# Two token blocks of a Strassen-Winograd mixture kernel taken as plain block products, with the weights' sums made afterwards and the fetches in another order

## The chip, the cores and the metric

One Trainium2 chip, and one core of it. The metric is the device time of one execution in microseconds (us), lower is better, as the median of three runs. Engine names are those of the profile: PE multiplies matrices, DVE, ACT and POOL work elementwise, SP issues the transfers.

## What is computed

Three layers follow one another. The first is an attention without softmax, over 8 batches of 8 heads with 576 tokens of 64 values; the other two are dense layers over the 4608 tokens that come out of it.

```python
kv  = einsum('bhsd,bhse->bhde', k, v)
out = einsum('bhsd,bhde->bhse', q, kv)
x   = out / sqrt(mean(out * out, -1) + 1e-6) * g_norm      # to 4608 x 512
h   = x @ w_in                                             # 512 -> 2048
x   = (maximum(h, 0) + alpha * minimum(h, 0)) @ w_out      # 2048 -> 512
out = ((x @ w_a) * (x @ w_b)) @ w_out2                     # 512 -> 1536 -> 512
```

All of it is in 32-bit floats, and the weights reach the chip as 64-bit floats.

## The kernel before, in words

**Products.** Every operand of the dense layers is split in two parts (a rounded one, and what rounding left), and one product of two 128-wide pieces is three matmuls (lines 610 to 613): rounded by rest, rest by rounded, rounded by rounded. On top of that the layers use Strassen and Winograd's scheme: a 2 x 2 block product takes seven products instead of eight, for which sums of the blocks are made of the weights (S1 to S4, lines 504 to 508) and of the tokens (`X.operands`, lines 549 to 585), and the results are added up again outside PE (`first`, lines 590 to 703).

**Units and blocks.** A weight is cut in units of 256 columns: w_in has eight, us1, and they are used in four pairs. The tokens are cut in nine blocks of 512 in the first layer. V (line 805) lists the work: the first layer's nine blocks, each with its four pairs, then the same for w_out and the last layer. One entry of a block and a pair is a piece, and pieces are numbered in the order of V. In the first layer a piece is 7 products x 2 units x 2 halves of the inner dimension x 3 = 84 matmuls of 256 columns, all on line 611.

**A unit's way before its first use.** `Unit.fetch` (line 474) brings 1 MB of 64-bit words in two transfers. `to_float` (line 267) turns each half to floats in one step on ACT (L276), four on DVE (L280, L281, L283, L284) and one on POOL (L286). `combine` (line 501) makes the four sums on DVE (L507), rounds all seven blocks on ACT (L514) and takes the rest on DVE (L516). Only then can PE use the unit. Units of the later weights go the same way, but are stored as floats in device memory by `convert` (line 462) and loaded again by `build` (line 490).

**Attention.** A step is two pairs of heads of one batch; there are 16 steps, and steps 2b and 2b+1 make batch b. On PE a step is `kv` (lines 320, 321), `out` (337, 342) and, after the norm on ACT and DVE (`norm`, line 353), `tr` (390, 394), which puts the tokens in the layout of the dense layers. Steps 0 and 1 leave the first block's tokens in the buffer x[0] and x[1]; the others go through the device-memory tensors xd, from which `X.load` (line 534) fetches a block.

**What sets the order.** Nothing runs in the order of the code. Each operation is a task with an engine, a cost (table COST, line 53), what it reads and writes, and a priority, which is a planned time in us. `Plan.order` (line 120) plays the tasks through on paper and writes down one fixed list for each engine; on the chip each engine takes its list strictly in turn. Transfers are all in SP's list, and one that waits for a buffer or for data holds back those behind it. The priorities come from constants: START is the planned time of the first product, STEP_AT and FETCH_AT place the first four steps and the eight fetches, STEP_IN names the pieces among which the other twelve steps are put, ATT, URGENT, PRELU, BUILD, CONVERT say how much ahead of its use a thing is to be done.

Of the kernel before, what the change touches and what calls it, by code (L numbers as in the profile page):

```python
# [19 lines left out]
P = 128  # L20
# [18 lines left out]
START = 36.0  # L39
ATT = 20.0  # L40
STEP_IN = [2 + 2 * i for i in range(12)]
NFIRST = 4
STEP_AT = [0, 5, 24, 34]
FETCH_AT = [-1, 2, 8, 14, 20, 26, 32, 38]
BUILD, CONVERT = 14.0, 10.0
PRELU = 8.0
PIECES = 2
LAST = 2.5
URGENT = 20.0
# [7 lines left out]
COL128 = 260  # L57
# [20 lines left out]
class Task:  # L78
    __slots__ = ("opts", "fn", "prio", "left", "users", "ready", "end", "eng")


class Plan:
# [37 lines left out]
    def order(self):  # L120
# [10 lines left out]
        out = []  # L131
        while True:
# [12 lines left out]
            x = heapq.heappop(can[e])[1]  # L145
            free[e] = x.end = s + x.opts
# [8 lines left out]
        assert len(out) == len(self.tasks)  # L155
# [4 lines left out]
def body(ctx: ExitStack, tc, kvm, kvt, qt, gn, w_in, alpha, w_o1, w_a, w_b, w_o2, outT):  # L160
# [134 lines left out]
    class Step:  # L295
# [17 lines left out]
        def kv(self, tag):  # L313
# [8 lines left out]
            for s in range(2):  # L322
                task("t", 5 * COL128, lambda s=s: products(s), self.prio, [(self.m[s], 0), (self.tt[s], 0)],
                     [(ps, s)])
# [4 lines left out]
        def out(self, tags):  # L329
# [15 lines left out]
            for s in range(2):  # L345
                task("t", 4 * COL128, lambda s=s: main(s), pr, z + [(self.q[s], 0)], [(p[s], 0)])
                task("a", 512, lambda s=s: nc.scalar.copy(self.o.t[0:CH, s, 0:4], p[s].t[0:CH]), pr, [(p[s], 0)],
                     [(self.o, s)])
            task("t", 2 * COL128, rest, pr, z + [(self.q[0], 0), (self.q[1], 0)], [(p[2], 0)])
# [33 lines left out]
        def tr(self, tags, x=None):  # L383
# [27 lines left out]
            for s in range(2):  # L411
                if x:
# [3 lines left out]
                    dma(32768, lambda s=s: xd[b].t[:, hp + s, 512:SEQ], lambda s=s: y[s].t[:, 512:SEQ], pr,  # L416
# [13 lines left out]

    class Unit:
# [3 lines left out]
        def __init__(self, w, f0, need, second=False):  # L435
            self.w, self.f0, self.need, self.closed, self.dram, self.second = w, f0, need, False, None, second
            self.ab = (1, 512) if second else (2, 256)
# [44 lines left out]
        def direct(self, prio, pieces=1):  # L482
            t = self.words
            self.c = sb("stg", [P, 8, 2, P], 2)
            for i in range(2):
                to_float(*self.cut[i], lambda i=i: self.dst(i), self.permute, [(t, 3 * i), (t, 1), (t, 2)],
                         (self.c, i), prio)
            self.combine(prio, pieces)

        def build(self, key, prio, pieces):  # L490
            self.key = key
            self.c = sb("stg", [P, 8, 2, P], 2)
            for i in range(2):
                dma(262144, lambda i=i: self.dst(i), lambda i=i: self.fit(self.dram.t[:, i]), prio,
                    [(self.dram, i)], [(self.c, i)])
            self.combine(prio, pieces)

        def dst(self, i):
            return self.c.t[:, 4:8:2] if i else self.c.t[:, 0::7]

        def combine(self, prio, pieces=1, engines="v"):
# [4 lines left out]
            for o, f, a, b, r in ops:  # L506
                sub(256, lambda e, o=o, f=f, a=a, b=b: getattr(e, f)(c.t[:, o], c.t[:, a], c.t[:, b]), prio,  # L507
                    r, [(c, {S1: "S1", S2: "S2", S3: "S3", S4: "S4"}[o])], engines)
            reads = [x0, x1, (c, "S1"), (c, "S2"), (c, "S3"), (c, "S4")]
            self.h = slot(self.key, [P, 2, 7, 2, P], F32R)  # L510
            self.pieces = [slice(0, 4), slice(4, 7)] if pieces > 1 else [slice(0, 7)]
            for s in self.pieces:
                k = (s.stop - s.start) * 256
                task("a", k, lambda s=s: nc.scalar.copy(self.h.t[:, 0, s], c.t[:, s]), prio, reads,  # L514
                     [(self.h, s.start)])
                sub(k, lambda e, s=s: e.tensor_sub(self.h.t[:, 1, s], c.t[:, s], f32(self.h.t[:, 0, s])), prio,  # L516
                    reads + [(self.h, s.start)], [(self.h, -1 - s.start)], "v")

        def parts(self, i):
            s = next(s for s in self.pieces if s.start <= i < s.stop)  # L520
            return [(self.h, s.start), (self.h, -1 - s.start)]


    class X:
# [9 lines left out]
        def load(self, prio):  # L534
            t1st, n1 = T1ST[self.la], T1ST[self.la] // 2
            src, size = (x2d, T2ND) if self.la else (xd, SEQ)
            for r in range(2):
                xf, t0, done = self.x[r], self.b * t1st, 0
                while done < t1st:
                    p, o = divmod(t0 + done, size)  # L540
                    m = min(t1st - done, size - o)
# [5 lines left out]
                    done += m  # L547

# [38 lines left out]
    opened = set()  # L587
    RIGHT = [0, 2, 1, 6, 3, 4, 5]

    def first(k, la, units, js, x, odd, late):  # L590
# [9 lines left out]
        def prod(i, bk, new=False):  # L600
# [3 lines left out]
            for u in range(2):  # L604
                w = units[u]

                def go(u=u, w=w):
                    ct = c.t.rearrange("p (m b k t) -> p m b k t", m=m_, b=2, k=2)[:, z]
# [120 lines left out]
    def second(k, la, b, j, n, unit, bk):  # L729
# [20 lines left out]
        for o, i in enumerate(ORDER):  # L750
            def go(i=i):
                for m in range(2):
# [59 lines left out]
    for vi, (la, b, ps) in enumerate(V):  # L812
        for j in (ps if ps is not None else range(8 if la == 0 else 6)):
            pieces.append((vi, j, t))
            t += UNIT2 if ps is None else PAIR[la]
# [5 lines left out]
    for pi, (vi, j, t) in enumerate(pieces):  # L821
        la, b, ps = V[vi]
        for u in ((pairs1, us2)[la][j] if ps is not None else [(wo1, wo2)[la][j]]):
            if u not in need:
# [43 lines left out]
    x.operands(START - 8)  # L868
    for i in range(8):
        us1[i].direct(us1[i].need - 8, 2 if i < 2 else 1)  # L870
# [17 lines left out]
    for pi, (vi, j, t) in enumerate(pieces):  # L888
        la, b, ps = V[vi]
        fst = pi == 0 or pieces[pi - 1][0] != vi  # L890
        if ps is not None:
            units = (pairs1, us2)[la][j]
            end = first(t, la, units, [2 * j, 2 * j + 1] if la == 0 else [j], x, pi % 2,
                        pi > max(at_time.values()) + 2)
# [10 lines left out]
        if pi + 1 < len(pieces) and pieces[pi + 1][0] != vi and V[vi + 1][2] is not None:  # L905
# [3 lines left out]
            x.operands(tn - 9)  # L909
# [32 lines left out]
    for x in plan.order():  # L942
# [47 lines left out]
```

## Time and profile before

| what | us |
|---|---|
| median of the three runs | 1714.66 |
| lowest and highest of them | 1713.45, 1715.16 |
| the profiled execution | 1713.24 |
| span of the profiled execution, first to last instruction | 1711.5 |
| PE busy in the span | 1642.0 (96%) |
| DVE busy in the span | 1331.7 (78%) |
| ACT busy | 750.0 (44%) |
| mean granted PE clock | 0.983 |

The profile is of one execution, and 1.74 us of its time lie outside the span. Times in its rows are counted from the start of the span. A fp32 matmul of the attention shows as two records; a matmul of the products as one. A matmul's busy time overlaps that of the next, so what one costs in a row of them is read from start to start.

### The profile page before, as it was taken

Reading aid. Unit: us, or ns where it says so; the run is one execution under the profiler, and the core shown is the slowest. Engines: PE = TensorE matmul, PEld = TensorE weight load, DVE = VectorE, ACT = ScalarE, POOL = GpSimd, SP = SyncE. Lnnn points to the kernel's source line nnn. Section 1 sums busy time; section 2 is a strip of 40 time slices with the busy share of each in tenths; the row PEclk is TensorE's granted clock in tenths of the full one; section 3 lists DMA queues with packets and bytes.
Section 4 is the critical chain, followed back from the end, with each engine's and each line's share of the span. In section 5 each row is a group of like instructions: output and inputs, shape, how many; then the busy total and the mean of one; then the engine's idle time right before and its main releaser. Section 6 shows DMA issues by size and latency. Waiting matters only on the chain.

```text
span 1711.5 us, 30160 instructions
## 1 busy us (share of the span) xinstructions
PE 1642.0 (96%) x12142; PEld 1632.4 (95%) x12142; DVE 1331.7 (78%) x1789; ACT 750.0 (44%) x929; POOL 153.5 (9%) x105
## 2 busy tenths in 40 slices
PE   5679999999999999999999999999999999999998
PEld 4669999999999999999999999999999999999998
DVE  6886667767769999988898776786667778887885
ACT  4555565556456433333344333333344334333332
POOL 1331012212100000000000101100101100000000
PEclk8789999999999999999999999999999999999999
DMA  8654478665536545445544443342444434444442
GB/s 250 216 174 142 163 237 260 219 223 189 207 124 222 164 158 179 156 159 182 175 137 154 141 164 130 121 163 91 147 142 148 160 130 136 136 148 136 149 136 75
DMA packets 179788, 279.87 MB, mean 164 GB/s; under 512 B 17088, under 2 KB 97472, under 8 KB 179648
## 3 DMA queue, kind: packets, MB, share of 16 engines
q1 hardware_dynamic: 179648, 277.94, 49.3%
q8 instruction: 95, 1.56, 0.4%
q14 instruction: 45, 0.37, 0.1%
HBM read 170.93 MB, written 106.95 MB: 162 GB/s over the span
## 4 chain that ended last, share of the span: by engine, by line
PE 68%; DVE 2%; issue 1%; ACT 1%; DMA 0%; DVEq 0%; ACTq 0%
PE banks L754 34%; PE banks L611 34%; DVE rops L747 1%; DVE fa L776 0%; DVE rl L747 0%; DVE fa L737 0%; ACT rops L571 0%; DVE w L516 0%; DMA fl<-gd 0%; DVE w L737 0%; ACT rops L746 0%; DVE fl L583 0%; ACT fa L621 0%; DVE stg L507 0%; ACT fa L685 0%
## 5 line engine op out<-in xcount | busy, mean ns | idle before, releaser
L611 PE MATMUL banks<-rops,w 128*128 128x256 f32 (+1 forms) x4752 | 701.9, 306 | 22.4 <-ACT w L514 7.2
L611 PEld LDWEIGHTS banks<-rops,w 128*128 128x128 f32 x4752 | 677.3, 193 | 27.2 <-ACT w L514 7.6
L754 PE MATMUL banks<-rops,w 128*128 128x256 f32 x3528 | 432.5, 283 | 3.7 <-DVE rops L747 3.1
L754 PEld LDWEIGHTS banks<-rops,w 128*128 128x128 f32 x3528 | 426.6, 191 | 4.7 <-DVE rops L747 2.9
L621 ACT COPY fa<-banks 128x768 f32<-128x768 f32 (+1 forms) x216 | 156.8, 729 | 334.0 <-PE banks L611 329.3
L611 PE MATMUL banks<-rl,w 128*128 128x384 f32 x1296 | 241.1, 340 | 0.9 <-ACT fa L621 0.9
L611 PEld LDWEIGHTS banks<-rl,w 128*128 128x128 f32 x1296 | 229.4, 188 | 1.2 <-ACT fa L621 1.2
L754 PE MATMUL banks<-rl,w 128*128 128x256 f32 x1764 | 217.5, 280 | 2.2 <-DVE rl L747 1.2
L754 PEld LDWEIGHTS banks<-rl,w 128*128 128x128 f32 x1764 | 212.1, 188 | 2.8 <-DVE rl L747 1.4
L625 DVE TENSOR_TENSOR fa<-fa,banks 128x768 f32<-128x768 f32 (+1 forms) x144 | 127.2, 884 | 77.4 <-PE banks L611 64.7
L746 ACT CAST rops<-fa 128x1792 fp32r<-128x1792 f32 x60 | 101.6, 1696 | 173.3 <-PE banks L754 85.5
L286 POOL TENSOR_TENSOR stg<-stg 128x512 f32<-128x512 f32 x52 | 81.6, 1570 | 958.1 <-DVE stg L284 689.8
L747 DVE TENSOR_TENSOR rops<-fa,rops 128x1792 fp32r<-128x1792 f32 x60 | 124.4, 2077 | 31.1 <-ACT rops L746 31.0
L737 DVE TENSOR_TENSOR fa<-fa 128x256 f32<-128x256 f32 (+1 forms) x267 | 132.8, 520 | 2.5
L689 DVE TENSOR_TENSOR fa<-fa 128x768 f32<-128x768 f32 x72 | 70.9, 985 | 37.1 <-ACT fa L621 36.4
L746 ACT CAST rl<-fa 128x1792 fp32r<-128x1792 f32 x29 | 49.0, 1690 | 108.0 <-PE banks L754 44.3
L685 ACT ACTIVATE fa<-banks,sal_sb 128x512 f32<-128x512 f32 x72 | 46.0, 684 | 93.3 <-PE banks L611 93.3
L697 DVE SCALAR_TENSOR_TENSOR fa<-banks,sgn_sb,fa 128x512 f32<-128x512 f32 x72 | 53.6, 747 | 41.3 <-ACT fa L685 41.0
L697 DVE SCALAR_TENSOR_TENSOR fa<-fa,sgn_sb 128x512 f32<-128x512 f32 x72 | 62.0, 883 | 29.0 <-ACT fa L685 29.0
L516 DVE TENSOR_TENSOR w<-stg,w 128x1792 fp32r<-128x1792 f32 (+2 forms) x50 | 71.2, 1441 | 10.6 <-ACT w L514 10.5
L747 DVE TENSOR_TENSOR rl<-fa,rl 128x1792 fp32r<-128x1792 f32 x29 | 58.7, 2024 | 20.5 <-ACT rl L746 20.5
L514 ACT CAST w<-stg 128x1792 fp32r<-128x1792 f32 (+2 forms) x50 | 59.3, 1211 | 22.9 <-DVE stg L507 18.3
(90 smaller groups left out, 1395.8 us busy)
## 6 DMA issues: line engine op xcount, KB each, us to landing
fa<-gd SPq DMA_DIRECT2D x178, 256.0 KB, 3.0
gd<-fa SPq DMA_DIRECT2D x144, 256.0 KB, 2.2
gd<-fa SPq DMA_DIRECT2D x72, 384.0 KB, 2.6
fl<-gd SPq DMA_DIRECT2D x64, 256.0 KB, 3.0
kvm<-in_kvm_dram SPq DMA_DIRECT2D x32, 448.0 KB, 4.7
stg<-in_w_o_dram SPq DMA_DIRECT2D x28, 512.0 KB, 4.4
wd<-stg SPq DMA_DIRECT2D x52, 256.0 KB, 2.3
stg<-wd SPq DMA_DIRECT2D x52, 256.0 KB, 3.6
```

The lines of the kernel that those rows point to most:

```text
L286: task("p", n, lambda: nc.gpsimd.tensor_add(out(), permute(f32(a())), permute(f32(u()))), prio, [A, U], [dst])
L514: task("a", k, lambda s=s: nc.scalar.copy(self.h.t[:, 0, s], c.t[:, s]), prio, reads, [(self.h, s.start)])
L516: sub(k, lambda e, s=s: e.tensor_sub(self.h.t[:, 1, s], c.t[:, s], f32(self.h.t[:, 0, s])), prio, reads + [(self.h, s.start)], [(self.h, - ...
L611: nc.tensor.matmul(bk.t[:, u, 0:n1], w.h.t[:, a, i, kk, :], ct[:, b, kk, :], start=bool(new and kk == 0 and m == 0 and (la or u == 0)), st ...
L621: task("a", 2 * n1, lambda: nc.scalar.copy(H.t[:, :, q], bk.t[:, :, 0:n1]), k + pos * dt - URGENT, both(bk), hq(q))
L625: task("v", 2 * n1, lambda: nc.vector.tensor_add(to.t if to else H.t[:, :, q], H.t[:, :, q], bk.t[:, :, 0:n1]), k + pos * dt - URGENT, bot ...
L689: task("v", t1st, lambda s=s: nc.vector.tensor_mul(h(0, s), h(0, s), h(1, s)), t, pv + [(H, (1, 2 * s)), (H, (1, 2 * s + 1))], pv)
L697: task("v3", t1st, lambda src=src, to=to, out=out, fc=fc: nc.vector.scalar_tensor_tensor(out(), src(), sgn_sb[:, fc:fc + 1], to(), ALU.mul ...
L737: d = lambda f, lo, hi, a, c, w: task("v", (hi - lo) * N2, lambda: nc.vector.tensor_sub(s.t[:, lo:hi], a(), c()), k - 9, f, w)
L746: task("a", 7 * N2, lambda: nc.scalar.copy(half(0), s.t[:, 0:7]), k - 7, reads, [(c, 0)])
L747: sub(7 * N2, lambda e: e.tensor_sub(half(1), s.t[:, 0:7], f32(half(0))), k - 7, reads + [(c, 0)], [(c, 1)], "v")
L754: nc.tensor.matmul(bk[i].t[:, m], unit.h.t[:, a, i, m, :], half(e)[:, SECOND[i]], start=bool(j == 0 and m == 0 and z == 0), stop=bool(j == ...
```

## The change

The first PLAIN = 2 blocks of the first layer (pieces 0 to 7) no longer use the seven products. The function `plain` multiplies the blocks as they are: 2 column halves s x 2 inner halves r x 2 x 3 matmuls for each unit, 48 matmuls of 512 columns in a piece, each unit and column half in a PSUM bank of its own (banks 0 to 3). The function of layer one (line 685's and line 697's pair of operations) then reads the bank once.

For that, `Unit.direct` only rounds and splits the four blocks as they come (ACT L520, DVE L522: A11 and A21, then A12 and A22, A21 in the place of S2) and stores them to device memory. `Unit.finish` loads them again before block 2, and then makes the four sums and writes the places 1 to 3 and 5 of the unit. `X.plain` splits a block's tokens without sums (ACT L605, DVE L606).

The planner gets a higher cost for the attention's matmuls (COLF = 540 in place of COL128 = 260), and it may put matmuls of the identity into a bank that is not in use (`warm`, L1049) where its own list leaves PE idle for more than 1 us before FILL = 150 us. Most constants are new, and with them all lists.

```diff
+PLAIN_PAIR = 48 * (512 + 32) / 2400
+PLAIN = 2
+STORE = 0
-START = 36.0
-ATT = 20.0
-STEP_IN = [2 + 2 * i for i in range(12)]
+START = 32.7
+ATT = 5.0
+STEP_IN = [2, 4, 6, 8, 10, 11, 13, 16, 18, 20, 21, 24]
...
-FETCH_AT = [-1, 2, 8, 14, 20, 26, 32, 38]
+FETCH_AT = [-1, 0, 13.7, 5.6, 26.0, 28.0, 31.1, 47.8]
...
+            if e == "t":
+                if s - free[e] > IDLE and s < FILL:
+                    n = int((s - free[e] - 0.5) / WARM / (1 if out else 1.6))
...
+        def direct(self, prio):
...
+            for i, pos in enumerate(((A11, 1), (A12, A22))):
+                to = lambda a, i=i: self.h.t[:, a, 4 * i:5 + 2 * i:1 + i] if i else self.h.t[:, a, 0:2]
+                task("a", 512, lambda i=i, to=to: nc.scalar.copy(to(0), dst(c, i)), prio, [(c, i)],
+                     [(self.h, z) for z in pos])
+                sub(512, lambda e, i=i, to=to: e.tensor_sub(to(1), dst(c, i), f32(to(0))), prio,
+                    [(c, i)] + [(self.h, z) for z in pos], [(self.h, -1 - z) for z in pos], "v")
+                dma(262144, lambda i=i: self.fit(self.dram.t[:, i]), lambda i=i: dst(c, i), prio + STORE, [(c, i)],
+                    [(self.dram, i)])
...
+        def finish(self, prio):
+
+            self.load(prio)
+            self.sums(prio)
+            for lo, hi in ((1, 4), (5, 6)):
+                self.halves(lo, hi, prio)
...
+    def plain(k, units, js, x, odd):
...
+                for r in range(2):
+                    def go(w=w, s=s, r=r, bk=bk):
+                        for kk in range(2):
+                            for m, (a, b) in enumerate([(0, 1), (1, 0), (0, 0)]):
+                                nc.tensor.matmul(bk.t, w.h.t[:, a, PLACES[s, r], kk, :], x.c[r].t[:, b, kk],
...
+    def warm(n):
+
+        for _ in range(n):
+            nc.tensor.matmul(banks[:, spare[0], 0:P], ident, ident, start=True, stop=True, skip_group_check=True)
```

How the lists move is shown at three places. The first is PE's list around the first products. Before, from the first product on (L652 only clears a bank; L320 to L342 are the attention's step 2, L390 the `tr` of step 1; w_245 and w_370 are the first two units):

```order
L652 MATMUL banks<-rops,w_245 128x512
L611 MATMUL banks<-rops,w_245 128x256 x12
L320 MATMUL banks<-kvm_330 128x128 x4
L321 MATMUL banks<-kvt_344 128x128
L320 MATMUL banks<-kvm_351 128x128 x4
L321 MATMUL banks<-kvt_358 128x128
L611 MATMUL banks<-rops,w_370 128x256 x12
L337 MATMUL banks<-kvbd,q_346 112x128 x4
L337 MATMUL banks<-kvbd,q_366 112x128 x4
L342 MATMUL banks<-kvbd,q_346 128x128
L342 MATMUL banks<-kvbd,q_366 128x128
L390 MATMUL banks<-ident,o_113 128x112 x8
```

And after the change, at the same place (L343 to L365 are step 2, L413 and L417 the `tr` of step 1, w_266 and w_395 the first two units):

```order
L666 MATMUL banks<-rops,w_266 128x512 x12
L343 MATMUL banks<-kvm_428 128x128 x4
L344 MATMUL banks<-kvt_442 128x128
L666 MATMUL banks<-rops,w_395 128x512 x12
L360 MATMUL banks<-kvbd,q_278 112x128 x4
L360 MATMUL banks<-kvbd,q_456 112x128 x4
L365 MATMUL banks<-kvbd,q_278 128x128
L365 MATMUL banks<-kvbd,q_456 128x128
L413 MATMUL banks<-ident,o_113 128x112 x8
L417 MATMUL banks<-ident,o_113 128x128 x2
L1049 MATMUL banks<-ident 128x128 x26
L666 MATMUL banks<-rops,w_266 128x512 x12
```

The 24 matmuls that need only x[0] stand ahead of the `tr` of step 1, which makes x[1]; then come 26 of the identity, and the 24 that need x[1], of which the last row shows the first 12.

The second place is DVE's list where the eighth and last unit of w_in becomes ready, up to the row that ends it. Before (w_1121 is that unit, w_506 its words, stg_980 its floats, L625 and L697 the results of piece 2):

```order
L280 TENSOR_SCALAR w_506<-w_506 128x512
L625 TENSOR_TENSOR banks<-fa,banks 128x512
L281 SCALAR_TENSOR_TENSOR w_506<-w_506 128x512
L326 COPY kvbd<-banks 64x2x64
L283 TENSOR_SCALAR w_506<-w_506 128x512
L284 SCALAR_TENSOR_TENSOR w_506<-w_506 128x512
L697 SCALAR_TENSOR_TENSOR fa<-banks,sgn_sb,fa 128x512
L625 TENSOR_TENSOR fa<-fa,banks 128x2x256
L697 SCALAR_TENSOR_TENSOR fa<-banks,sgn_sb,fa 128x512
L507 TENSOR_TENSOR stg_980<-stg_980 128x256 x3
L697 SCALAR_TENSOR_TENSOR fa<-fa,sgn_sb 128x512 x2
L516 TENSOR_TENSOR w_1121<-stg_980,w_1121 128x1792
```

After (w_991 is the eighth unit and w_668 its words, L387 the norm of step 4, L606 the tokens of block 1, L675 the results of piece 2):

```order
L606 TENSOR_TENSOR rops<-fa,rops 128x1024
L303 TENSOR_SCALAR w_668<-w_668 128x512
L304 SCALAR_TENSOR_TENSOR w_668<-w_668 128x512
L306 TENSOR_SCALAR w_668<-w_668 128x512
L307 SCALAR_TENSOR_TENSOR w_668<-w_668 128x512
L387 TENSOR_REDUCE sm_975<-sq_963 128x10
L675 SCALAR_TENSOR_TENSOR fa<-banks,sgn_sb,fa 128x512
L387 TENSOR_REDUCE sm_975<-sq_985 128x10
L522 TENSOR_TENSOR w_991<-stg_914,w_991 128x512
L394 RECIPROCAL sm_975<-sm_975 128x20
L522 TENSOR_TENSOR w_991<-stg_914,w_991 128x2x256
```

The four sums and the long L516 are gone from this place; they stand later, as L563 and L554, among the results of block 1.

The third place is SP's list after the change, where the tokens of block 1 and block 2 are fetched (fa<-xd is `X.load`, gd<-fa a result, wd<-stg a unit's floats on their way out):

```order
L199 DMA xd_60<-y_891 128x576
L199 DMA gd_5_81<-fa 128x512
L199 DMA wd_121<-stg_914 128x2x256
L199 DMA kvm_965<-in_kvm_dram 112x1024
L199 DMA fa<-xd_60 128x2x128
L199 DMA kvt_987<-in_kvt_dram 128x256
L199 DMA kvm_989<-in_kvm_dram 112x1024
L199 DMA fa<-xd_60 128x2x448
```

The last row is the second half of block 1's tokens. It stands behind the first piece of block 2's tokens, which waits for the buffer that L606 above reads. Before, no store of a unit of w_in and no second load of one is in this list.

More of the change, by code (lines that the diff above doesn't have):

```diff
@@ L79, with after @@
     __slots__ = ("opts", "fn", "prio", "left", "users", "ready", "end", "eng")
+class Cold:
+    until = 0.0
+    def after(self, idle, now, cost):
+        if idle > 1.2:
+            self.until = now + 3.2
+        return min(cost, max(0.0, self.until - now) / 2)
 class Plan:
@@ L130, in order @@
                 place(x)
-        out = []
+        out, extra, cold = [], 0, Cold()
         while True:
@@ L145, in order @@
             x = heapq.heappop(can[e])[1]
+            if e == "t":
+                if s - free[e] > IDLE and s < FILL:
+                    n = int((s - free[e] - 0.5) / WARM / (1 if out else 1.6))
+                    y = Task()
+                    y.fn, y.eng, y.opts, y.end, y.prio, y.ready = lambda n=n: warm(n), e, n * WARM, s - 0.5, x.prio, 0
+                    out.append(y)
+                    extra += 1
+                    free[e] = s - 0.5
+                x.opts += cold.after(s - free[e], s, x.opts)
             free[e] = x.end = s + x.opts
@@ L490, in build, with load @@
+        def load(self, prio):
+            self.c = c = sb("stg", [P, 8, 2, P], 2)
+            for i in range(2):
+                dma(262144, lambda i=i: dst(c, i), lambda i=i: self.fit(self.dram.t[:, i]), prio,
+                    [(self.dram, i)], [(c, i)])
+        def finish(self, prio):
[3 more added lines that the diff above has]
+                self.halves(lo, hi, prio)
         def build(self, key, prio, pieces):
             self.key = key
-            self.c = sb("stg", [P, 8, 2, P], 2)
@@ L493, in build @@
[L493 to L501, printed above, removed]
+            self.load(prio)
+            self.sums(prio)
+            self.h = slot(self.key, [P, 2, 7, 2, P], F32R)
+            for lo, hi in [(0, 4), (4, 7)] if pieces > 1 else [(0, 7)]:
+                self.halves(lo, hi, prio)
@@ L502, in combine, with sums @@
+        def sums(self, prio):
             c = self.c
@@ L507, in combine @@
                 sub(256, lambda e, o=o, f=f, a=a, b=b: getattr(e, f)(c.t[:, o], c.t[:, a], c.t[:, b]), prio,
[L508 to L517, printed above, removed]
+                    r, [(c, {S1: "S1", S2: "S2", S3: "S3", S4: "S4"}[o])], "v")
         def parts(self, i):
-            s = next(s for s in self.pieces if s.start <= i < s.stop)
-            return [(self.h, s.start), (self.h, -1 - s.start)]
+            return [(self.h, i), (self.h, -1 - i)]
     class X:
@@ L823, in body @@
         for u in ((pairs1, us2)[la][j] if ps is not None else [(wo1, wo2)[la][j]]):
+            if vi < PLAIN:
+                u.plain = pi
+            elif la == 0 and ps is not None and not u.sums_need:
+                u.sums_need = t
             if u not in need:
@@ L892, in body @@
             units = (pairs1, us2)[la][j]
-            end = first(t, la, units, [2 * j, 2 * j + 1] if la == 0 else [j], x, pi % 2,
-                        pi > max(at_time.values()) + 2)
+            if vi < PLAIN:
+                end = plain(t, units, [2 * j, 2 * j + 1], x, pi % 2)
+                for u in units:
+                    if u.plain == pi:
+                        u.finish(u.sums_need - BUILD)
+            else:
+                end = first(t, la, units, [2 * j, 2 * j + 1] if la == 0 else [j], x, pi % 2,
+                            pi > max(at_time.values()) + 2)
         else:
```

93 lines of the change are left out of this document (71 added, 22 removed).

## The prediction

> **What bounds the kernel now.** I read the page's slices first, then PE by stages, then what PE waited for, then DVE. The page's second part cuts the span in 40 slices of 42.8 us; a digit is a tenth of the slice:
>
> ```profile
> span 1711.5 us, 30160 instructions
> ...
> PE   5679999999999999999999999999999999999998
> ...
> PEclk8789999999999999999999999999999999999999
> ```
>
> From the fourth slice on PE is full, at full clock. So whatever comes later is worth what it does to PE's work, and whatever shortens the first four slices moves everything behind it forward. Stages of that beginning (columns: window, its length, then busy us and count for PE, weight loads, DVE, ACT, POOL, then clock, DMA share, GB/s). The cuts are the first product, DVE's last operation on block 0's tokens, and, at 145.71, the end of the last wait:
>
> ```profile
> 0.00:36.12 36.12, 18.08 (x90) 17.12 (x90) 19.73 (x41) 14.46 (x26) 6.59 (x12) 0.91 0.80 245
> 36.12:58.15 22.03, 16.08 (x94) 14.98 (x95) 21.37 (x39) 14.55 (x28) 4.15 (x3) 0.74 0.94 296
> 58.15:99.00 40.85, 28.22 (x197) 27.13 (x197) 32.77 (x56) 19.00 (x32) 12.95 (x9) 0.76 0.54 170
> 99.00:145.71 46.71, 33.47 (x240) 31.66 (x239) 38.34 (x61) 24.30 (x40) 16.66 (x9) 0.85 0.47 147
> 145.71:199.20 53.49, 53.30 (x448) 53.03 (x447) 30.84 (x50) 29.63 (x53) 2.98 (x2) 1.00 0.45 152
> ```
>
> PE busy 16 of 22 us sounds fair, but the clock is 0.74 there, so its matmuls are slow ones. DVE is busy 97%, 80% and 82% in the three stages after the first product, and in the fifth, where PE is full, only 58%. PE's waits up to 145.71 name the units (w):
>
> ```profile
> PE banks L611 <- ACT w L514: 7.2, 2, 5.8
> ...
> PE banks L611 <- DVE w L516: 5.3, 4, 2.9
> PE banks L337 <- DVE kvbd L326: 5.2, 1, 5.2
> ```
>
> What PE lost follows from the price of its work at full clock, read from start to start in PE's timeline:
>
> ```profile
> 213.89 19.83 PE L611 MATMUL banks<-rops,w 128*128 128x256 f32 x162
> 233.56 1.05 PE L320 MATMUL banks<-kvm 112*128 112x128 f32 x8
> ...
> 308.64 1.05 PE L320 MATMUL banks<-kvm 112*128 112x128 f32 x8
> ...
> 309.67 6.37 PE L611 MATMUL banks<-rops,w 128*128 128x256 f32 x48
> 315.88 1.91 PE L337 MATMUL banks<-kvbd,q 128*112 128x128 f32 x16
> ...
> 317.99 0.96 PE L611 MATMUL banks<-rops,w 128*128 128x256 f32 x6
> 318.79 0.93 PE L390 MATMUL banks<-ident,o 112*128 112x112 f32 x8
> ...
> 319.70 14.04 PE L611 MATMUL banks<-rops,w 128*128 128x256 f32 x114
> ...
> 419.90 0.40 PE L652 MATMUL banks<-rops,w 128*128 128x512 f32 x1
> 420.13 3.04 PE L611 MATMUL banks<-rops,w 128*128 128x256 f32 x24
> ```
>
> A matmul of 256 columns costs 19.67/162 = 0.1214 us, one of 512 columns 0.23 (one case). An attention step costs 2 x 1.03 for `kv`, 2.11 for `out`, 0.91 for `tr`. At 199.20 block 2 has just begun. By PE's list it has by then done 8 pieces x 84 = 672 matmuls, L652, eight `kv`, eight `out`, seven `tr`: 81.6 + 0.2 + 16.5 + 16.9 + 6.4 = 121.6 us. **Lost: 199.2 - 121.6 = 77.6 us.** All of it is waiting or slow clock, before 145.71.
>
> **PE's work changes.** A piece goes from 84 x 0.1214 = 10.2 to 48 x 0.23 = 11.0 us; eight pieces cost 6.7 us more. After the change block 2's first product stands behind 384 plain matmuls, nine `kv`, eight `out` and seven `tr`: 88.3 + 18.5 + 16.9 + 6.4 = 130.1 us. The state to compare with is the old kernel one `kv` later, 199.2 + 2.1 = 201.3.
>
> The Trainium skill has a rule here that would price the plain products otherwise: "TensorE: Matmul & The Clock Gate", section "Back-to-back issue gap", gives about 131 ns for a matmul of 512 columns in a sustained stream of weight loads and matmuls. By it the 384 would take an estimated 50 us and not 88. The trace does not agree: it has 230 ns.
>
> **DVE's work moves.** Between the bars stand the busy us of a group and the mean ns of one operation, up to 146 us:
>
> ```profile
> L507 DVE TENSOR_TENSOR stg<-stg 128x256 f32<-128x256 f32 x32 | 15.1, 475 | 1.5 <-POOL stg L286 1.5
> L516 DVE TENSOR_TENSOR w<-stg,w 128x1792 fp32r<-128x1792 f32 x6 | 12.1, 2009 | 0.8 <-ACT w L514 0.8
> L284 DVE SCALAR_TENSOR_TENSOR w<-w 128x512 f32<-128x512 uint32 x16 | 11.8, 746 | 0.1
> L281 DVE SCALAR_TENSOR_TENSOR w<-w 128x512 int32<-128x512 int32 x16 | 11.4, 720 | 0.1
> L364 DVE TENSOR_REDUCE sm<-sq 128x10 f32<-128x640 f32 x14 | 11.4, 813 | 3.4 <-ACT sq L362 3.4
> L280 DVE TENSOR_SCALAR w<-w 128x512 int32<-128x512 int32 x16 | 9.2, 581 | 8.7 <-ACT w L276 8.7
> L283 DVE TENSOR_SCALAR w<-w 128x512 int32<-128x512 int32 x16 | 7.5, 473 | 0.1
> L697 DVE SCALAR_TENSOR_TENSOR fa<-fa,sgn_sb 128x512 f32<-128x512 f32 x6 | 6.2, 1059 | 1.6 <-ACT fa L685 1.6
> L697 DVE SCALAR_TENSOR_TENSOR fa<-banks,sgn_sb,fa 128x512 f32<-128x512 f32 x6 | 4.5, 748 | 3.4 <-ACT fa L685 3.4
> ...
> L572 DVE TENSOR_TENSOR rops<-fa,rops 128x1024 fp32r<-128x1024 f32 x2 | 2.4, 1215 | 0.0
> L625 DVE TENSOR_TENSOR banks<-fa,banks 128x512 f32<-128x512 f32 x3 | 2.1, 696 | 4.5 <-PE banks L611 4.5
> ...
> L572 DVE TENSOR_TENSOR rops<-fa,rops 128x512 fp32r<-128x512 f32 x3 | 2.0, 662 | 0.0
> ```
>
> The old list makes the eighth unit ready at 144.24. DVE's busy time up to there:
>
> ```profile
> 0.00:20.00 20.00, 7.00 (x16) 1.00 0.93 269
> 20.00:58.15 38.15, 34.09 (x63) 0.76 0.81 262
> 58.15:144.24 86.09, 70.38 (x116) 0.81 0.50 155
> ```
>
> That is 111.5 busy and 32.8 idle: 13.0, 4.1 and 15.7. Ahead of the same point, the lists differ in this:
> - Each unit needed 2 x (0.581 + 0.720 + 0.473 + 0.746) = 5.04 for the floats, 4 x 0.475 = 1.90 for sums, 2.01 for the rest: 8.95. Now it needs 5.04 and two differences of 512, not in the trace in this form; the nearest row is L572's 0.662, and I take 0.7: 6.44. Eight units: 20.1 less.
> - The results of a piece took 2 x 0.696 + 2 x 0.748 + 2 x 1.059 = 5.0, and take 4 x 0.748 = 3.0 now. Three pieces stand ahead of the point in both: 6.0 less.
> - Block 0's tokens took six operations of 512 (three L572, three L558 priced alike) and three of 1024 (two L572, one L583): 4.0 + 3.6 = 7.6. Now three L606 at 1.215 stand there: 4.0 less.
> - The norm of one step fewer stands ahead: 2 x 0.813 = 1.6 less, and small operations that I leave out.
>
> Busy time to be done: 111.5 - 31.7 = 79.8. With only the early idle time (13.0 + 4.1) the eighth unit is ready at 97; with all the old idle time, 112.6. The idle time after 58 came mostly from PE being late (L625, L697, `kvbd`), and PE is less late now; with the small operations, **I take 100.**
>
> What left DVE's way is not gone: eight times four sums and the differences of 1024 columns (at L572's 1.215: 8 x (1.90 + 1.2) = 25 us) come between 100 and block 2. In that stretch old DVE was busy 58% (the fifth stage), so 67 us offer about 28 idle ones; block 2 also finds its pieces' results cheaper by 2.0 each. It fits, narrowly. If it did not, block 2 would wait for a unit, not the whole.
>
> **When block 2 can start.** Two chains meet. Behind the first use of the eighth unit PE's list has 216 matmuls, four `kv`, three `out`, three `tr` ahead of block 2: 49.7 + 8.2 + 6.3 + 2.7 = 66.9, so 100 + 67 = 167 (164 to 180). The other begins with x[1], which step 1 makes. Old DVE read it first here:
>
> ```profile
> 52.96 0.69 DVE L558 TENSOR_TENSOR fa<-fa 128x512 f32<-128x512 f32 x1
> ```
>
> The steps' chain up to there is unchanged. One rounding on ACT and L606's 1.2 follow, with some queueing: operand at 56.5. PE has by then done three `kv`, three `out`, two `tr` and 24 matmuls, 19.8 us, so 110.3 remain: again 167. Two chains that fit so tightly will cost stalls; between none and the 13.2 idle us of the old fourth stage I take 4. **Block 2 starts at 171, and 201.3 - 171 = 30 us are gained.**
>
> The rest on one answer each. The identity matmuls stand only where the list has PE idle; the first 34 start when POOL has written the identity, take 34 x 0.21 (a fifth of 1.03) = 7 to twice that when slow, and end near 11, while the first `kv` could run at 8.2 but then slowly. Cost 0, and up to 5 us if they run slow throughout. The stores and second loads are 2 x 16 x 256 KB = 8.4 MB, 28 us of DMA at 296 GB/s, beside PE's work.
>
> **After block 2** PE's work is the same, and of its waits from 145 on these are the largest and the smallest of eight rows, 13.6 us in sum:
>
> ```profile
> PE banks L611 <- DVE fa L697: 3.4, 1, 3.4
> ...
> PE banks L754 <- DVE fa L697: 0.4, 1, 0.4
> ```
>
> The new constants reorder this too. I leave the sum at 13.6, with 7 less or 6 more as bounds. So the profiled execution goes from 1713.24 (span 1711.5 and 1.7 around it) to 1683; the median lies 1.4 above the profiled one, hence **1684**.
>
> **Rivals.**
> - DVE keeps its idle share (0.16). Five lists taken strictly in turn leave gaps for each other. The eighth unit comes at 112, block 2 at 180 + 4, gain 17: 1697.
> - The later waits shrink by half as well (0.07): 1677.
> - Wide matmuls are cheaper than the one case shows, a rule by which a matmul costs what 256 columns cost (0.02). Then 216 x 0.109 = 23 us more are gained behind the eighth unit: 1661. The 0.23 speaks against it. The rule of the Trainium skill's page named above goes in this direction.
> - The gain is given back behind block 2 (0.04): the conversions of w_out and the attention have 30 us less time, DVE becomes the bound, and the time stays within 0.2%. Against it: 58% in the fifth stage.
> - Slower, by SP's list (0.05). The second half of block 1's tokens stands behind a piece of block 2's, which waits for L606; that waits for the first half. Up to block 2's second operand the rows of the new list add up to 41.6 MB. At the 200 GB/s that the old kernel reaches by 145.71 (its four stages weighted) this is 208 us, and some 6 more to the product: 214 and not 201.3, so 1727. It decides below 213 GB/s. Against it: 245 and 296 GB/s in the first two stages, where there was more to fetch.
>
> **The numbers.** The forecast (1676 to 1692) has 0.66. The range 1672 to 1700 takes in the second and most of the first rival. About 0.2% (3.4 us) is what a measurement can tell: faster 0.91, same 0.04, slower 0.05.
>
> **What would show it.** Right: block 2's first L704 at 165 to 177, the eighth unit's L522 at 97 to 105, x[1]'s L606 by 57, clock near 1 in the first 100 us, 512-column matmuls 0.23 apart. Wrong: a start of block 2 beyond 185, DVE idle more than 20 us before its eighth unit, PE waiting for DMA, or PE waits after block 2 that have grown by 10 us.

## The result, and the profile after

| | before | after |
|---|---|---|
| median, four runs each on one chip | 1714.06 us (1711.38 to 1715.16) | 1674.09 us (1673.88 to 1675.41) |
| profiled execution | 1713.24 | 1674.15 |
| span, mean granted PE clock | 1711.5, 0.983 | 1672.4, 0.999 |

The ratio is 0.977, with a 95% interval of 0.975 to 0.979: 40 us faster.

The page's slices after the change. No slice of PE is short of a nine but the last, and none of its clock:

```profile
span 1672.4 us, 30100 instructions
...
PE   9999999999999999999999999999999999999998
...
PEclk9999999999999999999999999999999999999999
```

The same stages as before (window, its length, busy us and count of PE, weight loads, DVE, ACT, POOL, then clock, DMA share, GB/s):

```profile
0.00:36.12 36.12, 33.49 (x274) 33.17 (x275) 22.93 (x45) 14.97 (x27) 9.53 (x14) 1.00 0.94 282
36.12:58.15 22.03, 20.83 (x143) 18.45 (x143) 20.88 (x38) 14.57 (x30) 6.54 (x5) 1.00 1.05 311
58.15:99.00 40.85, 40.85 (x234) 35.32 (x233) 36.87 (x63) 24.98 (x45) 16.63 (x12) 1.00 0.89 282
99.00:145.71 46.71, 46.71 (x259) 40.26 (x258) 29.01 (x55) 23.20 (x43) 7.79 (x6) 1.00 0.83 269
145.71:199.20 53.49, 53.07 (x394) 49.84 (x393) 42.91 (x73) 31.53 (x57) 7.21 (x5) 1.00 0.73 233
```

The clock is 1.00 in all five stages. DVE is busy 9 us less in the fourth stage (29.01 for 38.34) and 12 us more in the fifth (42.91 for 30.84). The weights' sums (L563) now stand in these two, with 6.9 us in the fourth and 8.6 in the fifth. The transfers run at 233 to 311 GB/s where 147 to 296 were. PE's column is not to be read as useful work: one group of it is filler, the matmuls of the identity.

```profile
L1049 PE MATMUL banks<-ident 128*128 128x128 f32 x238 | 30.4, 291 | 1.4 <-POOL ident masks.py:199 1.4
```

What tells more is when things stand where in PE's timeline (start, length, count):

```profile
48.22 5.97 PE L1049 MATMUL banks<-ident 128*128 128x128 f32 x52
55.16 5.75 PE L666 MATMUL banks<-rops,w 128*128 128x512 f32 x24 [0.97 <-DVE rops L606]
...
68.86 13.88 PE L666 MATMUL banks<-rops,w 128*128 128x512 f32 x60
82.58 0.55 PE L413 MATMUL banks<-ident,o 112*128 112x112 f32 x4
...
166.96 1.68 PE L704 MATMUL banks<-rops,w 128*128 128x256 f32 x12
```

Block 1's tokens let PE go on at 55.16; 60 plain matmuls take 13.72 us to the next row's start, 0.2287 us each; block 2 starts at 166.96. In DVE's timeline the tokens of x[1] (L606) and the two last differences of the eighth unit (L522) are:

```profile
53.89 1.21 DVE L606 TENSOR_TENSOR rops<-fa,rops 128x1024 fp32r<-128x1024 f32 x1
...
95.94 0.68 DVE L522 TENSOR_TENSOR w<-stg,w 128x512 fp32r<-128x512 f32 x1
...
96.73 0.63 DVE L522 TENSOR_TENSOR w<-stg,w 128x512 fp32r<-128x512 f32 x1
```

The unit is ready at 97.36 where it was 144.24. DVE up to that point, in the prediction's stretches (DVE is the third busy column):

```profile
0.00:20.00 20.00, 18.35 (x139) 18.19 (x140) 8.19 (x19) 5.36 (x9) 5.35 (x11) 1.00 0.91 276
20.00:58.15 38.15, 35.97 (x279) 33.43 (x278) 35.62 (x66) 24.19 (x47) 10.72 (x8) 1.00 1.02 303
58.15:97.36 39.21, 39.21 (x226) 33.99 (x225) 35.76 (x60) 24.98 (x45) 16.30 (x11) 1.00 0.89 278
```

It is busy 79.6 us and idle 11.8, 2.5 and 3.5. From there to block 2 it is busy 44.9 of 69.6 us, so what left its way has room, and no wait of PE for a unit of w_in is among those below, in the rows shown or left out. What PE still waited for up to 165 us (total, times, longest; five rows, 3.9 in sum) names no weight:

```profile
PE banks L1049 <- POOL ident masks.py:199: 1.4, 1, 1.4
PE banks L417 <- DVE kvbd L349: 1.0, 1, 1.0
PE banks L666 <- DVE rops L606: 1.0, 1, 1.0
```

and behind 165 us there are seven rows, 8.9 in sum where 13.6 were; the first and the last:

```profile
PE banks L704 <- DVE fa L718: 2.2, 5, 1.4
...
PE banks L704 <- ACT fa L778: 0.4, 1, 0.4
```

So of the 39.1 us by which the profiled execution is shorter, 201.3 - 166.96 = 34.3 are gained at block 2's start and 13.6 - 8.9 = 4.7 behind it. By the prediction's prices PE has lost 166.96 - 130.1 = 36.9 us when block 2 starts, for 77.6 before.

### The profile page after: what moved, and what is told of

It reads as the page before. It is cut to its first block, busy times and chain, and to the rows that moved or that the text cites. A ratio compares the mean times of both kernels' runs of the same rounds, so it can differ in the third digit from the quotient of the medians.

```text
span 1672.4 us, 30100 instructions
## 1 busy us (share of the span) xinstructions
PE 1653.6 (99%) x12092; PEld 1631.1 (98%) x12092; DVE 1316.9 (79%) x1783; ACT 740.6 (44%) x921; POOL 154.4 (9%) x105
## 4 chain that ended last, share of the span: by engine, by line
PE 91%; DVE 5%; issue 1%; ACT 1%; DMA 1%; SPq 0%; DVEq 0%; POOL 0%; ACTq 0%; POOLq 0%
PE banks L704 46%; PE banks L848 35%; PE banks L666 5%; PE banks L360 1%; PE banks L343 1%; PE banks L1049 1%; DVE fa L790 1%; DVE rops L840 1%; PE banks L413 1%; DMA fa<-xd 0%; PE banks L365 0%; ACT fa L778 0%; PE banks L344 0%; DVE w L554 0%; DVE stg L563 0%
## 5 line engine op out<-in xcount | busy, mean ns | idle before, releaser
L704 PE MATMUL banks<-rops,w 128*128 128x256 f32 (+1 forms) x4080 | 606.8, 306 | 3.5 <-DVE fa L718 2.2
L704 PEld LDWEIGHTS banks<-rops,w 128*128 128x128 f32 x4080 | 586.9, 190 | 6.8 <-DVE fa L718 3.7
L848 PEld LDWEIGHTS banks<-rops,w 128*128 128x128 f32 x3528 | 426.9, 191 | 3.7 <-DVE rops L840 2.1
L714 ACT COPY fa<-banks 128x768 f32<-128x768 f32 (+1 forms) x200 | 148.0, 741 | 326.7 <-PE banks L704 313.3
L718 DVE TENSOR_TENSOR fa<-fa,banks 128x768 f32<-128x768 f32 (+1 forms) x136 | 121.8, 896 | 74.1 <-PE banks L704 69.7
L309 POOL TENSOR_TENSOR stg<-stg 128x512 f32<-128x512 f32 x52 | 87.5, 1683 | 978.7 <-DVE stg L307 729.1
L666 PE MATMUL banks<-rops,w 128*128 128x512 f32 x384 | 92.6, 395 | 1.0 <-DVE rops L606 1.0
L666 PEld LDWEIGHTS banks<-rops,w 128*128 128x128 f32 x384 | 70.6, 188 | 15.0 <-DVE rops L606 1.2
L554 DVE TENSOR_TENSOR w<-stg,w 128x768 fp32r<-128x768 f32 (+3 forms) x56 | 67.3, 1220 | 13.8 <-ACT w L552 13.8
L790 DVE SCALAR_TENSOR_TENSOR fa<-banks,sgn_sb,fa 128x512 f32<-128x512 f32 x56 | 41.9, 748 | 33.2 <-ACT fa L778 32.4
L790 DVE SCALAR_TENSOR_TENSOR fa<-fa,sgn_sb 128x512 f32<-128x512 f32 x56 | 49.6, 921 | 19.3 <-ACT fa L778 19.1
```

The lines of the kernel that those rows point to most:

```text
L309: task("p", n, lambda: nc.gpsimd.tensor_add(out(), permute(f32(a())), permute(f32(u()))), prio, [A, U], [dst])
L554: sub(k, lambda e: e.tensor_sub(self.h.t[:, 1, lo:hi], c.t[:, lo:hi], f32(self.h.t[:, 0, lo:hi])), prio, reads + [(self.h, z) for z in at] ...
L666: nc.tensor.matmul(bk.t, w.h.t[:, a, PLACES[s, r], kk, :], x.c[r].t[:, b, kk], start=(r == 0 and kk == 0 and m == 0), stop=(r == 1 and kk ...
L704: nc.tensor.matmul(bk.t[:, u, 0:n1], w.h.t[:, a, i, kk, :], ct[:, b, kk, :], start=bool(new and kk == 0 and m == 0 and (la or u == 0)), st ...
L714: task("a", 2 * n1, lambda: nc.scalar.copy(H.t[:, :, q], bk.t[:, :, 0:n1]), k + pos * dt - URGENT, both(bk), hq(q))
L718: task("v", 2 * n1, lambda: nc.vector.tensor_add(to.t if to else H.t[:, :, q], H.t[:, :, q], bk.t[:, :, 0:n1]), k + pos * dt - URGENT, bot ...
```

## The experiments

The question was not whether block 2 starts earlier but why. The change does two things at once: it takes sums out of DVE's list ahead of the eighth unit, and it makes all lists anew (constants, the cost of attention's matmuls, the identity). With the identity comes a small rule of the planner, `cold.after` in the diffs: it charges PE extra time after a planned idle stretch of more than 1.2 us.

Theory A says that the first of the two, DVE's shorter list, is the cause; its rivals are the clock (C) and the new lists (B); D and E came when both A and B had missed, and F, G and H are told with their runs.

"Old lists" and "new lists" below mean the planner's constants and costs: only the run that gives DVE's work back keeps the rows of the change in place, and in all others the planner makes its own lists. Every time stands beside runs of the kernel before on the same chip, whose median was 1714.0 to 1714.6.

This table says where each profiled execution lost its time; the last column is its time less the two before it. "Compared" means that attention steps are added until as many stand ahead of block 2 as in the change: 1.0 us (half a step's `kv`) after block 2's first product in the kernel before, and 5.1 (one step's `kv`, `out` and `tr`) after 182.70 and 167.92 in the two runs with seven products in new lists.

| kernel | median us | profiled us | block 2 starts | PE's waits behind 165 us | rest |
|---|---|---|---|---|---|
| before | 1714.1 | 1713.24 | 201.3 (compared) | 13.6 | 1498.3 |
| the change | 1674.1 | 1674.15 | 166.96 | 8.9 | 1498.3 |
| no identity | 1678.2 | 1680.46 | 172.07 | 9.3 | 1499.1 |
| plain blocks, old lists | 1705.6 | 1704.85 | 190.72 | 16.5 | 1497.6 |
| DVE more | 1692.2 | 1692.41 | 185.26 | 8.9 | 1498.3 |
| old cost | 1692.3 | 1692.55 | 178.88 | 13.5 | 1500.2 |
| old start | 1679.2 | 1679.35 | 170.38 | 9.3 | 1499.7 |
| old rest | 1682.8 | 1682.69 | 165.75 | 19.1 | 1497.8 |
| plain, true cost | 1696.1 | 1695.17 | 177.32 | 18.8 | 1499.1 |
| before, true cost | 1710.6 | 1711.52 | 197.88 | 15.3 | 1498.3 |
| seven products, new lists | 1693.8 | 1694.93 | 187.8 (compared) | 8.4 | 1498.7 |
| the same without the weights' sums | 1675.9 | 1680.54 | 173.0 (compared) | 8.3 | 1499.2 |
| one plain block | 1678.5 | 1678.24 | 169.46 | 9.9 | 1498.9 |

The rest is the same within 2.6 us, so these two numbers tell a kernel's time. Where block 2 starts behind 165 us, a wait just ahead of it is counted in both columns; that is 1.5 us for the old cost and 0.5 or less for the others.

**No identity matmuls.**

```diff
-                if s - free[e] > IDLE and s < FILL:
+                if False:
```

> The changed kernel (1674.1) without the matmuls of the identity; no other row of the lists moves. Theory A (the time came from DVE: what a unit and the tokens need before their first product became shorter) expects these matmuls to cost nothing and to bring little, since they stand where PE has nothing to do: 1674 to 1679. Theory C (the time came from the clock: the old PE was busy 96 us up to 145.71 with work that costs 68 us at full clock) expects most of those 28 us back: 1690 to 1700.

1678.2 us, ratio 0.979 (0.977 to 0.980), 4.1 more than the change. The second and third stage:

```profile
36.12:58.15 22.03, 13.55 (x84) 11.43 (x84) 20.77 (x37) 14.53 (x30) 5.72 (x4) 0.91 0.94 291
58.15:99.00 40.85, 40.20 (x222) 34.34 (x222) 34.66 (x56) 22.91 (x42) 15.20 (x11) 0.96 0.82 269
```

The clock falls to 0.91 and 0.96 there, and the whole edit is worth 4 of the 40 us: A's number holds, and theory C falls in the form that the identity bought the time. Both clocks are still above the 0.74 and 0.76 of the kernel before, so that a PE which waits less also runs faster is not excluded. The 4 us are not the identity's alone, and the expectation errs in saying that no other row moves. Without the identity the planned idle stretches are longer, `cold.after` charges for them, and the lists differ from the first products on (PE's has 6 matmuls on L666 and then `kv`, where the change has `kv` and then 12).

**Seven products in the new lists.** PLAIN = 0: no plain block, and the weights' sums where they were, but all constants, costs and the identity of the change.

```diff
-PLAIN = 2
+PLAIN = 0
...
-    x.plain(START - 8)
+    x.operands(START - 8)
```

> All new constants, the new cost of the attention's matmuls, the new order of fetches and the matmuls of the identity, but seven products with sums for all blocks (no plain ones, no stores and second loads). Theory A expects DVE to have about 32 us more to do ahead of the eighth unit, so most of the gain gone: 1698 to 1710. Theory B (the time came from the better lists, above all from the attention's true cost) expects most of it to stay: 1678 to 1688.

1693.8 us, ratio 0.988 (0.987 to 0.990): between both expectations. The new lists alone give 20 us, and the plain blocks another 20. The third stage:

```profile
58.15:99.00 40.85, 35.84 (x296) 34.41 (x296) 39.88 (x66) 20.02 (x32) 14.64 (x10) 1.00 0.45 142
```

DVE is busy 39.88 of 40.85 us. The new lists have filled it, and more than full it cannot be.

**Two plain blocks in the old lists.** The constants and the cost of before, no identity and no `cold.after`. One cost stays that of the change: `tr` is taken at 250 columns, before at 260.

```diff
-START = 32.7
-ATT = 5.0
+START = 36.0
+ATT = 20.0
...
-COLF, COL128 = 540, 250
+COLF, COL128 = 260, 250
...
-                x.opts += cold.after(s - free[e], s, x.opts)
```

> The reverse: two plain blocks, with the old constants, the old cost of the attention's matmuls, the old order of fetches and no matmuls of the identity. Theory A expects most of the gain: 1680 to 1690. Theory B expects little: 1700 to 1712. If both parts are needed together, this and the kernel with all blocks in seven products both lie in between, about 1690 to 1700.

1705.6 us, ratio 0.995 (0.993 to 0.996): only 8 to 9 us. A falls as the whole story. The third stage, and the largest of DVE's waits from 30 to 125 us:

```profile
58.15:99.00 40.85, 32.57 (x139) 25.89 (x139) 27.54 (x44) 16.85 (x32) 13.60 (x10) 0.83 0.60 189
```

```profile
DVE fa L674 <- ACT fa L672: 19.4, 11, 3.9
```

Here DVE has little to do and stands idle 13 of 41 us. It waits for results (L674 takes one in after ACT has read the bank) that PE has not yet made (ACT's L672 waits 30.9 us for PE's L665 in the same stretch), and the next unit's steps stand behind them in its list. PE is late as well: the eighth unit is ready at 117.28, but the 216th matmul ahead of block 2, its first use, stands at 126.44. The two single parts add up to 20 + 9 us and not to 40: some 10 us come only when both are there.

**DVE's work given back.** Each L522 of the change is done three times, in the same lists.

```diff
-                sub(512, lambda e, i=i, to=to: e.tensor_sub(to(1), dst(c, i), f32(to(0))), prio,
+                sub(512, lambda e, i=i, to=to: [e.tensor_sub(to(1), dst(c, i), f32(to(0))) for _ in range(3)], prio,
```

> The changed kernel with the same lists, but each L522 (the rest of a unit's blocks, 16 of them) is done three times on DVE with the same result: 32 x 0.65 = 21 us more on DVE ahead of the eighth unit. Theory A (DVE's list sets when units are ready) expects PE to wait for w, less the few us that DVE is idle: 1684 to 1693. A theory by which the fetches, or the attention's steps, set the pace of the first 100 us expects little: 1674 to 1679.

1692.2 us, ratio 0.987 (0.986 to 0.989): 18.1 more, as A said. DVE's last L522 of the eighth unit, and PE's first matmul of block 2:

```profile
116.40 2.08 DVE L522 TENSOR_TENSOR w<-stg,w 128x512 fp32r<-128x512 f32 x3
```

```profile
185.26 1.68 PE L704 MATMUL banks<-rops,w 128*128 128x256 f32 x12
```

The unit is ready at 118.48; the 66.9 us that the prediction put between it and block 2 lead to 185.4, and 185.26 is measured. DVE is busy 102.8 us up to that point for 79.6 in the change, the unit is 21.1 us later and the time 18.1 longer, so in these lists DVE's work reaches the end nearly whole.

**One number of the cost table.**

```diff
-COLF, COL128 = 540, 250
+COLF, COL128 = 260, 250
```

> The two single parts gave 20.8 and 9 us, both together 40; with plain blocks and old lists DVE waited 19 us for results of PE (L674 behind L672) that stood ahead of the next unit's work in its list. Theory D: the old planner took an attention matmul for half of its true cost, so it put the results of a piece too early in DVE's list, and PE and DVE waited for each other in turn; then giving back the old cost alone, all else as changed, must lose much: 1684 to 1700. Rival E (the new constants matter, the cost hardly): 1672 to 1680.

1692.3 us, ratio 0.987 (0.984 to 0.990): 18.2 more than the change, as D said, by a number that stands in no instruction. Its last L522 and its filler up to 200 us:

```profile
111.68 0.68 DVE L522 TENSOR_TENSOR w<-stg,w 128x512 fp32r<-128x512 f32 x1
```

```profile
L1049 PE MATMUL banks<-ident 128*128 128x128 f32 x338 | 41.8, 285 | 1.4 <-POOL ident masks.py:199 1.4
```

The planner takes `kv` and `out` for half as long as they are and orders the lists for a PE that the chip does not have. The eighth unit comes at 112.36, 15 us later, and block 2 at 178.88. PE's waits up to 165 us are 3.9 in sum as in the change, since 100 more identity matmuls stand where they were: with filler, the list of waits no longer shows the loss.

**The other constants,** in two parts: START, STEP_AT and FETCH_AT of before, then ATT, STEP_IN, BUILD, CONVERT, PRELU, LAST and URGENT of before.

```diff
-START = 32.7
+START = 36.0
...
-STEP_AT = [0, 17.3, 8.0, 43.4]
-FETCH_AT = [-1, 0, 13.7, 5.6, 26.0, 28.0, 31.1, 47.8]
+STEP_AT = [0, 5, 24, 34]
+FETCH_AT = [-1, 2, 8, 14, 20, 26, 32, 38]
```

> The changed kernel with the old START, STEP_AT and FETCH_AT, that is the old order of the first four steps and of the fetches. Theory D expects little: 1674 to 1681. Rival E, in the form that the order of fetches and steps matters: 1684 to 1700.

1679.2 us, ratio 0.980 (0.977 to 0.982): 5.1 more, as D expected, most of it at block 2's start (170.38).

```diff
-ATT = 5.0
+ATT = 20.0
...
-BUILD, CONVERT = 11.6, 33.3
-PRELU = 12.7
+BUILD, CONVERT = 14.0, 10.0
+PRELU = 8.0
...
-LAST = 3.5
-URGENT = 14.7
+LAST = 2.5
+URGENT = 20.0
```

> The changed kernel with the old ATT, STEP_IN, BUILD, CONVERT, PRELU, LAST and URGENT. URGENT was 20 and is 14.7: results stood 5 us earlier in the lists. Theory D expects a part: 1678 to 1688, some 5 of it as waits after block 2 (old 13.6, new 8.9). Rival E, in the form that these constants matter: 1690 to 1705.

1682.8 us, ratio 0.982 (0.979 to 0.984): 8.7 more, again within D's numbers, though D put only some 5 of it behind block 2. Block 2 starts at 165.75, even earlier than in the change. The loss is all behind it (19.1 for 8.9); the largest waits there:

```profile
PE banks L848 <- DVE rops L840: 7.4, 5, 2.1
PE banks L704 <- DVE banks L718: 3.4, 2, 1.8
```

**Plain blocks in the old lists, with the true cost.** The run of plain blocks and old lists once more, with COLF = 540.

```diff
-COLF, COL128 = 260, 250
+COLF, COL128 = 540, 250
```

> Plain blocks with all old constants and no matmuls of the identity (1705.6), but with the attention's true cost in the planner. Theory D expects most of the way to the changed kernel without these matmuls (1678.2): 1683 to 1692. Rival E expects 1698 to 1707.

1696.1 us, ratio 0.989 (0.986 to 0.992): 9.5 gained by the cost, between both expectations: D's "most of the way" fails. The constants and the identity with its rule are the other 22 us.

**The true cost in the kernel before.**

```diff
-                task("t", 5 * COL128, lambda s=s: products(s), self.prio, [(self.m[s], 0), (self.tt[s], 0)],
+                task("t", 5 * 540, lambda s=s: products(s), self.prio, [(self.m[s], 0), (self.tt[s], 0)],
```

and the same in the two tasks of `out`.

> The kernel before with one number changed: the planner takes the matmuls of kv and out at 540 columns' cost in place of 260. Theory D (the old lists were planned with attention's matmuls at half their cost, and this counts whether the blocks are plain or not): about the 9.5 us that the same edit gave to the two plain blocks with the old constants: 1701 to 1709. Rival G (with seven products DVE is 80 to 97% busy after the first product, and no order of PE's list helps while DVE is the one that is late): 1711 to 1717.

1710.6 us, ratio 0.998 (0.997 to 0.999): 3.4 gained, between D's numbers and G's and nearer to G's. The third stage:

```profile
58.15:99.00 40.85, 32.36 (x226) 31.30 (x225) 37.63 (x60) 20.62 (x34) 11.45 (x8) 0.78 0.56 174
```

DVE is busy 37.63 of 40.85 us (32.77 before), and the eighth unit is ready at 145.74, no earlier than the 144.24 of before. That with seven products a better order soon meets a full DVE is read from these two figures and was not tested apart.

**Seven products without the weights' sums,** with the constants and costs of the change. PLAIN is 0, the units are rounded and split as for plain blocks but not stored and loaded again, and each product reads one of the four blocks in place of a sum. The kernel leaves out the sums and three of seven splits, so it does not compute the layer's result.

```diff
...
+    WRITTEN = [0, 1, 0, 4, 4, 6, 6]
...
-                            nc.tensor.matmul(bk.t[:, u, 0:n1], w.h.t[:, a, i, kk, :], ct[:, b, kk, :],
+                            nc.tensor.matmul(bk.t[:, u, 0:n1], w.h.t[:, a, i if la else WRITTEN[i], kk, :], ct[:, b, kk, :],
```

> The change with seven products in all nine blocks of the first layer, as in the run with PLAIN = 0, but the eight units of w_in are only rounded and split as plain blocks are, and each product takes one of the four blocks where it should take a sum: the four sums and three of the seven splits are left out of DVE's and ACT's work, and PE's work is that of seven products. DVE has about 22 us less to do in the first 130 us (17.4 of sums, 16.3 of L548 against 11 to 12.6 of L522). Theory A (the weights' sums in DVE's list are what seven products lose): the loss of 20 us against the change goes, and PE's work is 6.7 us less than the change's: 1667 to 1680. Rival H (it is the tokens' sums, the results' additions or PE's narrow matmuls that hold the seven products up, not the weights): at most a third of it comes back, 1687 to 1694.

1675.9 us, ratio 0.978 (0.976 to 0.980); the profiled execution was the longest of its four, 1680.5. Of the 19.7 us between the change and its form with seven products 17.9 are back: the weights' sums and the splits of them are what the plain blocks were good for. The edit takes their rounding off ACT as well, but the run that gives work back to DVE alone costs as much. Its third stage:

```profile
58.15:99.00 40.85, 37.75 (x313) 36.76 (x313) 36.59 (x59) 22.05 (x40) 15.21 (x10) 0.99 0.51 158
```

DVE is at 36.59, as in the change (36.87). PE's 6.7 us less of work do not show in the time. PE waits 11.9 us up to 165 here for 3.9 in the change, 4.6 of them for the transfers of `kvm`; what the tokens' sums, the additions and the lists have in that was not taken apart.

**One and three plain blocks.**

```diff
-PLAIN = 2
+PLAIN = 1
```

> The change with one plain block in place of two. Theory A (in the first 150 us DVE's list sets the pace, and every block taken plainly takes sums out of that list): the sums of the weights come back ahead of block 1, so the time lies between the change with seven products (1693.8) and the change (1674.1): 1679 to 1689. Rival F (the last part of the gain is in the first block alone, since the eight units are ready by 97 us whichever way block 1 is taken): PE saves the 3.4 us that the second plain block costs and the time is 1669 to 1675.

```diff
-PLAIN = 2
+PLAIN = 3
```

> The change with three plain blocks. Theory A: PE waits for only 3.4 us in the first 165 us of the changed kernel, so there is almost nothing left to win, and a third plain block costs 3.4 us of PE's work: 1675 to 1680. Rival F (the sums still hold PE up after block 2): the later start of the sums gives 3 us or more beyond the cost, 1667 to 1674.

1678.5 us (0.979, 0.977 to 0.980) and 1684.4 us (0.982, 0.980 to 0.984). Neither meets an expectation: one block is 4.4 worse than two, just below A's range, three are 10.3 worse and above both. With three, 3.4 are PE's work and 5.5 are waits behind 165 us (14.4 for 8.9); two of these:

```profile
PE banks L848 <- DVE rops L840: 6.1, 5, 2.0
PE banks L343 <- ACT y L432: 2.1, 2, 1.1
```

The constants were kept, and they are those for two blocks; what one or three would be worth with their own stays open. No run was faster than the change.

## Why the prediction came out right, and where its reasons did not

The time, 1674.1, lies inside the range of 1672 to 1700 but below the 1676 to 1692 to which most of the chance was given. The forecast was 1684. Of the 10 us between, 4.0 are block 2's start (171 forecast, 166.96 measured), 4.7 the waits behind it (13.6 kept, 8.9 measured), and 1.5 the median, which was put 1.4 above the profiled execution and lies 0.06 below it.

The runs with both the cost and the plain blocks varied make a table of medians:

| lists | seven products | two plain blocks | plain blocks give |
|---|---|---|---|
| old constants, old cost | 1714.0 | 1705.6 | 8.4 |
| old constants, true cost | 1710.6 | 1696.1 | 14.5 |
| new constants, true cost, identity | 1693.8 | 1674.1 | 19.7 |
| the lists give | 20.2 | 31.5 | |

- **What bounds the beginning:** right. DVE's list set the pace; giving back its work (+18.1) and taking the weights' sums and their splits away from seven products (-17.9) both show it.
- **DVE's work ahead of the eighth unit:** 79.8 forecast, 79.6 measured, though an L522 takes 0.790 in the mean and not 0.7. Its idle time was put at 17 to 20 and is 17.8; the unit is ready at 97.36, forecast 100.
- **PE's prices:** 0.23 forecast, 0.2287 over 60 matmuls, and the rival of cheaper wide matmuls fell with that. The Trainium skill's rule ("TensorE: Matmul & The Clock Gate", section "Back-to-back issue gap", some 131 ns for 512 columns) does not agree with these 228.7 ns; the measurement decides.
- **Two chains to block 2:** right in their tightness. The eighth unit is ready 1.6 us before PE comes to it (the 216th matmul from the end stands at 99.0, counting back through the 36 that begin at 92.09, 0.2287 us each), and block 1's tokens let PE go on at 55.16, 111.8 us before block 2; 110.3 were forecast. The term that was mis-sized is **the 4 us of stalls**: PE waited for nothing between 55.16 and 165, and block 2 came at 166.96 and not 171.
- **Waits behind block 2** left at 13.6: they are 8.9. The run with the old rest has 19.1 there, so the new constants are worth 10 us at that place. The prediction said that they reorder this and gave them no value; the bounds of 7 less and 6 more hold both.
- **The identity at no cost or gain:** the run without it is 4.1 longer, with lists that moved too.
- **Why DVE's idle time goes:** here the argument failed although its number held, and that is luck. The prediction let DVE's idle time shrink because less work makes PE less late, and gave the planner's new cost no term. DVE up to the moment at which the eighth unit is ready (length, busy us, clock, DMA share, GB/s), in the kernel before, with seven products in new lists, with plain blocks in old lists, and in the change:

```profile
0.00:144.24 144.24, 111.47 (x193) 0.82 0.64 199
0.00:126.93 126.93, 111.07 (x188) 0.99 0.73 219
0.00:117.28 117.28, 80.14 (x144) 0.85 0.79 246
0.00:97.36 97.36, 79.57 (x142) 1.00 0.94 287
```

The plain blocks take away 31 us of work in either lists, as forecast (31.7), and no idle time: it is 32.8 and 37.1 in the old lists, 15.9 and 17.8 in the new. The idle time went by the lists. The rival of an idle DVE (unit at 112, 1697 us) is near what the change would have been with the old cost alone: 112.36 and 1692.3. The plain blocks by themselves bring 8.4 us; the 40 come of both.

- **SP's list:** the change moves 282 GB/s in its third stage, above the 213 at which that rival decided, and PE waits for no transfer.
- **A reading of the trace:** the last wait of the beginning ends at 144.29 and not at 145.71, where the prediction's fourth stage ends; no sum rests on it.

That a unit's steps stand behind results which PE has not made (plain blocks in the old lists) is read from waits, not from a run that moved only these. Why the cost is worth 18.2 with the new constants and 9.5 with the old ones was not taken apart.

## What to carry to other kernels

Where one engine prepares data for another and both take fixed lists in turn, less work on the first pays in full only when the lists are made anew for it, with true costs: the parts here gave 8 and 20 us alone and 40 together. A wrong duration in a planner can cost as much as work does (18.2 us here, for 18.1 by 23 us more of DVE's work), so hold its cost table against the profile's own rows before tuning constants. And where idle time is filled with matmuls that compute nothing, judge by the time at which the first useful thing after it starts, not by busy share or waits.

## What the runs showed of the chip that was not expected

Identity matmuls in idle places went with a granted clock of 1.00 in the first five stages of the change, where the run without them shows 0.91 and 0.96 in the second and third; 4.1 us between the two are small beside the 30 us of filler. The filler does not hold the clock by itself, since it stands only where the plan has PE idle. With it the clock was still 0.92 in the second stage with seven products in new lists, and 0.92 and 0.96 in the third and fourth with DVE's work given back.

A plain piece of 48 matmuls with 512 columns costs PE little more than one of 84 with 256 (11.0 for 10.2 us by the measured prices). The 6.7 us that eight pieces of seven products save did not show: without the weights' sums they were no faster (1675.9 for 1674.1), since PE waited 8 us more.
